# Sinkhorn attention into a SwiGLU block on one core: unit pairs set further apart, and the unread matmuls at the start split in two

## The chip, the core and the metric

The kernel runs on one NeuronCore of a Trainium2 chip. A core has five engines with queues of their own: TensorE (PE, matrix multiply; its weight loads are listed as PEld), VectorE (DVE), ScalarE (ACT), GpSimd (POOL) and SyncE (SP, here only for DMAs). Matmuls write to PSUM, which has eight banks of 128 partitions by 512 fp32 values; ScalarE and VectorE read results from there. The metric is the device time of one launch in microseconds (us), lower is better, as the median of several executions. All times below are us unless marked ns.

## The reference

Four batches, eight heads, 768 positions, head size 64. Each head's sequence is cut into 8 blocks of 96. A small 8 x 8 matrix per head is normalised by five Sinkhorn rounds, and mixes the blocks of K and V. Attention then runs within each block only, and its output, 3072 tokens by 512 features, goes through a SwiGLU block with 1536 hidden features.

```
for _ in range(5):
    P = exp(P - max(P, -1)); P = P / sum(P, -1); P = P / sum(P, -2)
k_sorted = einsum('bhij,bhjcd->bhicd', P, k_blocks)      # v_sorted likewise
attn = softmax(scale * q_block @ k_sorted_block.T)
x = (attn @ v_sorted_block)  -> [3072, 512]
out = (silu(x @ w_gate) * (x @ w_val)) @ w_out
```

## The kernel before, in words

**Start.** V, Q and K of batch 0 are loaded by DMA. ScalarE and VectorE run the five Sinkhorn rounds (L184 to L200), each one exp on ScalarE and six small VectorE operations; the last multiply writes the mixing matrix `p_bf` (L203). Meanwhile TensorE has no real work. It runs matmuls whose result nobody reads: 115 of 32 x 32 (L417), one on V once V has landed (L420), and `fill` of 11 matmuls of 128x512 (L423). Then come the matmuls that transpose `p_bf` (`weights`, L429) and the mixing of V (`v_chunk`, tile `tv`) and of K and Q (`kq_chunk`, tile `tkq`) of batch 0. GpSimd and ScalarE have reordered V into `vch` before (`copy_v`, L116 to L120).

**Units.** A batch has 8 units, each of four blocks times two heads. A unit is: 8 score matmuls (`scores`, `qk`), an exp on ScalarE (`exps`, L289), 8 AV matmuls (`av`, L303), a reciprocal and a scaling multiply on VectorE (`r_sb` L307, `st` L309), and a transpose of `st` to `xt`. For batches 0 and 1 the transpose is four TensorE matmuls into `x_ps` (`xtr`, L320) and a VectorE copy; for batches 2 and 3 it is a DMA (`x_dma`). Units go in pairs: the first uses PSUM pair "b", the second pair "a", two banks each. A pair's AV uses the same banks as its scores, and so do the mixing matmuls of V, K and Q. A bank is written anew only after it was read.

**FFN blocks.** Half a batch of `xt` (384 tokens) is one block, `ffn(n)`, n = 0 to 7: 12 times a gate group (`g_ps`, four matmuls of 128x384) and a value group (`v_ps`, four). Behind a gate group ScalarE takes the tanh (L362) and VectorE multiplies (`gs_sb`, L364); behind a value group VectorE makes `h` (L377). The output matmuls of the block before (`outp`, `o_ps`, 12 of 128x512, in three parts of four) come after each fourth step; ScalarE copies `o_ps` to `o_sb` (L394) and SyncE writes it out. `g_ps`, `v_ps` and some `o_ps` share three "gen" banks in turn; other `o_ps` use one bank "x", which `x_ps` uses too (L386).

**Order.** TensorE's and GpSimd's queues are written by hand: `merge(main, side)` (L545) issues the FFN groups in order, adds up their nominal costs (0.65 for a gate or value group, 0.87 for a part of `o_ps`), and puts each side item behind the first group that brings the sum to the item's time. `units(b, us, ats)` (L522) makes the side items of pairs: scores at `at`, the exp of the second unit at `at + 1.3`, AV at `at + 2.0` and `at + 3.9`, the transposes 3.3 later. `kqs` and `vs` place the mixing of K, Q and V in the same way. VectorE's and ScalarE's orders in the FFN blocks are left to the framework's scheduler. On GpSimd, four copies of V of batch 1 into `vch` (L571 to L572) follow the DMA loads of weights, K, Q and V; every `v_chunk` matmul of batch 1 reads all of them.

Of the kernel before, what the change touches and what calls it, by code (L numbers as in the profile page):

```python
# [10 lines left out]
BF16 = mybir.dt.bfloat16  # L11
# [6 lines left out]
def kernel(  # L18
# [11 lines left out]
    nc = tc.nc  # L30

    B, H, S, D = q.shape
    NB = sort_net.shape[-1]
    C = S // NB
    BH = B * H
    H2 = H // 2
    scale = 1.0 / float(D) ** 0.5
    N_ITER = 5
# [15 lines left out]
    const = ctx.enter_context(tc.tile_pool(name="const", bufs=1))  # L54
# [58 lines left out]
    def copy_v(eng, pair, rows, s, n=4):  # L113
        cs = slice(s * (C // n), (s + 1) * (C // n))
        dst = vch3[rows, :, cs]
        src = v_tiles[pair][rows, cs, :]  # L116
        if eng is nc.scalar:
            eng.copy(dst, src.transpose([0, 2, 1]))
        else:
            eng.tensor_copy(dst, src.transpose([0, 2, 1]))  # L120
# [47 lines left out]
    id4 = ident.rearrange("p (u h j) -> p h u j", u=2, h=H)  # L168
    idq = ident[R:2 * R, R:2 * R].rearrange("p (g two j) -> p two g j", two=2, j=NB)

    rowred = const.tile([BH, NB, 1], FP32)
    colred = const.tile([BH, 1, NB], FP32)
    p_bf = const.tile([BH, NB, H, NB], BF16)
# [6 lines left out]
    def bank_tile(name, tag="gen"):  # L180
        return psum.tile([128, 512], FP32, name=name, tag=tag, bufs=3 if tag == "gen" else 1)

    p_ps = bank_tile("p_ps")[0:BH, 0:NB * NB].rearrange("p (i j) -> p i j", j=NB)
    for it in range(N_ITER):  # L184
        nc.scalar.activation(p_ps, p_sb if it == 0 else p_ps, AF.Exp)
        if it == 1:
            with nc.allow_low_precision("0/1 mask"):
                nc.vector.tensor_reduce(mask, id4, axis=AX.XY, op=ALU.add)
            nc.vector.tensor_copy(rmix[0][R:2 * R, :, 1, :, :], idq)
        if it == 2:  # L190
            copy_v(nc.scalar, 0, lowr, 2, 8)
        if it == 3:
            copy_v(nc.scalar, 0, lowr, 3, 8)
        nc.vector.reduce_sum(rowred[:, :, 0], p_ps, axis=AX.X)
        nc.vector.reciprocal(rowred, rowred)
        nc.vector.tensor_mul(p_ps, p_ps, rowred.to_broadcast([BH, NB, NB]))
        nc.vector.reduce_sum(colred[:, 0, :], p_ps.transpose([0, 2, 1]), axis=AX.X)
        nc.vector.reciprocal(colred, colred)
        if it < N_ITER - 1:
            nc.vector.tensor_mul(p_ps, p_ps, colred.to_broadcast([BH, NB, NB]))  # L200
# [8 lines left out]
    def drain(eng, dst, src):  # L209
        if eng == "v":  # L210
            nc.vector.tensor_copy(dst, src)  # L211
        else:
            nc.scalar.copy(dst, src)  # L213
# [48 lines left out]
    def scores(b, u, tag):  # L262
        half, g = divmod(u, H2)
        k_sb, k_at, q_sb, q_at = ((kqts[b], 0, kqts[b], GI * C) if b < 2 else
                                  (kqts["p"], (b - 2) * GI * C, kqts["q"], (b - 2) * GI * C))
        if tag == "gen":
            wide = None
            pss = [bank_tile("qk"), bank_tile("qk")]
        else:
            wide = pair_tile("qk", tag).rearrange("p (two n) -> p two n", two=2)  # L270
            pss = [wide[:, 0], wide[:, 1]]
        for i4 in range(4):
            at = (g * NB + half * 4 + i4) * C
            for two in range(2):
                lo = two * D
                nc.tensor.matmul(pss[two][:, i4 * C:(i4 + 1) * C],  # L276
                                 lhsT=k_sb[lo:lo + D, k_at + at:k_at + at + 128],
                                 rhs=q_sb[lo:lo + D, q_at + at:q_at + at + C],
                                 start=True, stop=True)
        return wide, pss  # L280
# [11 lines left out]
    def qk(b, u, tag="b"):  # L292
        exps(b, u, *scores(b, u, tag))
# [19 lines left out]
    def xt_tile(tag, n):  # L313
        bank = psum.tile([128, 1024], BF16, name="x_ps", tag=tag, bufs=3 if tag == "gen" else 1)
        return bank[:, 0:n * 4 * C].rearrange("p (g a b) -> p g a b", g=n, b=C)

    def x_to(dst, b, u):
        st = sts.pop((b, u))
        for i4 in range(4):
            nc.tensor.transpose(dst[:, i4, :], st[:, i4].rearrange("p a b -> p (a b)"),  # L320
                                ident[0:C, 0:C])

    def xtr(b, u):
        half, g = divmod(u, H2)
        if g == 0:
            xts[(b, half)] = xtp.tile([128, H2, TW], BF16, name=f"xt{b}_{half}", tag="xt")
        x_ps = xt_tile("x", 1)[:, 0]
        x_to(x_ps, b, u)
        return xts[(b, half)][:, g, :], x_ps.rearrange("p a b -> p (a b)")
# [20 lines left out]
    def gate(n, m):  # L350
        xt = xts[divmod(n, 2)]
        g_ps = psum.tile([128, TW], FP32, name="g_ps", tag="gen", bufs=3)
        for kc in range(NKC):
            nc.tensor.matmul(g_ps, lhsT=wg_sb[:, kc, ts(m, 128)], rhs=xt[:, kc, :],  # L354
                             start=(kc == 0), stop=(kc == NKC - 1))
        gate_out(n, m, g_ps)
# [23 lines left out]
    o_tiles = {}  # L380

    def outp(n, t3, part):
        b, half = divmod(n, 2)
        h_w = h_tiles[n]
        if part == 0:
            o_tiles[n] = bank_tile("o_ps", "x" if 2 <= n < 2 * B - 1 or n == 2 * B - 1 and t3 == 0 else "gen")  # L386
        o_ps = o_tiles[n]
        for m in range(part * 4, part * 4 + 4):
            nc.tensor.matmul(o_ps, lhsT=h_w[:, m, ts(t3, 128)], rhs=wo_sb[:, m, :],  # L389
                             start=(m == 0), stop=(m == NFC - 1))  # L390
        if part < 2:
            return
        o_sb = opool.tile([128, DM], FP32, name="o_sb", tag="o_sb")
        nc.scalar.copy(o_sb, o_ps)  # L394
        base = b * S + half * TW + t3 * 128
        nc.sync.dma_start(out=out[ds(base, 128), :], in_=o_sb)
# [14 lines left out]
    idle_ps = bank_tile("idle_ps", "x")  # L411

    def fill(tile, n):
        for _ in range(n):
            nc.tensor.matmul(tile, lhsT=warm_sb[:, 0:128], rhs=warm_sb, start=True, stop=True)

    for _ in range(115):  # L417
        nc.tensor.matmul(idle_ps[0:32, 0:32], lhsT=warm_sb[:, 0:32], rhs=warm_sb[:, 0:32],
                         start=True, stop=True)
    nc.tensor.matmul(idle_ps[:, 0:128], lhsT=ident[lowr, :],  # L420
                     rhs=v_tiles[0][lowr, 0:2, :].rearrange("p c d -> p (c d)"),
                     start=True, stop=True)
    fill(idle_ps, 11)  # L423

    w_ps = bank_tile("w_ps")[:, 0:NB * B * H].rearrange("p (i b h) -> p i b h", b=B, h=H)

# [48 lines left out]
    idle_ps = bank_tile("idle_ps")  # L475
# [46 lines left out]
    def units(b, us, ats):  # L522
        us = list(us)
        todo = []
        for n, at in enumerate(ats):
            u, u2 = us[2 * n:2 * n + 2]
            held = []
            todo.append((at, lambda u=u, u2=u2, held=held: (qk(b, u, "b"), held.append(scores(b, u2, "a")))))
            todo.append((at + 1.3, lambda u2=u2, held=held: exps(b, u2, *held[0])))
            for w, tag, t in ((u, "b", 2.0), (u2, "a", 3.9)):  # L530
                if b < 2:
                    todo.append((at + t, lambda w=w, tag=tag: av(b, w, tag)))
                    todo.append((at + t + 3.3, lambda w=w: drain("v", *xtr(b, w))))
                else:
                    todo.append((at + t, lambda w=w, tag=tag: (av(b, w, tag), x_dma(b, w))))
        return todo
# [5 lines left out]
    def vs(f, size, ats):  # L542
        return [(at, lambda m=m: f(1, m * size, size, "sv"[m % 2], "ba"[m % 2])) for m, at in enumerate(ats)]

    def merge(main, side):  # L545
        done, k = 0.0, 0
        side = sorted(side, key=lambda t: t[0])
        for c, f in main:
            f()
            done += c  # L550
            while k < len(side) and side[k][0] <= done:
                side[k][1]()
                k += 1
        while k < len(side):
            side[k][1]()
            k += 1

    def ffn(n):
        todo = []
        for m in range(NFC):  # L560
            if n > 0 or m > 1:
                todo.append((0.65, lambda m=m: gate(n, m)))
            if n > 0 or m > 0:
                todo.append((0.65, lambda m=m: value(n, m)))
            if n > 0 and m % 4 == 3:
                for part in range(3):
                    todo.append((0.87, lambda m=m, part=part: outp(n - 1, m // 4, part)))
        return todo
# [7 lines left out]
    q_cast(3)  # L576
    both = slice(0, 128)
    kq1 = kqs(1, (11.8, 1.3, 5.2))
    merge(ffn(0), units(0, range(4, 8), (0.0, 5.2)) + kq1[:1])
    merge(ffn(1), kq1[1:] + vs(v_chunk, 16, (8.6, 9.4, 10.2, 11.0)) + units(1, range(4), (11.2, 15.0)))  # L580
    for s in range(4):
        copy_v(nc.gpsimd, 1, both, s)
    nc.vector.memset(kqt_tile("p")[:, 2 * GI * C:], 0.0)
# [42 lines left out]
```

## Time and profile before

| What | us |
|---|---|
| median of 11 executions | 257.08 (255.89 to 259.81) |
| the profiled execution | 256.89 |
| its span, first to last instruction | 254.7 |
| `g_ps` matmuls (L354), 376 records at 326 ns | 76.5 busy |
| `v_ps` matmuls (L372), 380 records at 326 ns | 77.3 busy |
| `o_ps` matmuls (L389), 256 records at 379 ns | 62.0 busy |
| tanh on ScalarE (L362), 96 at 491 ns | 47.1 busy |
| `gs_sb` on VectorE (L364), 96 at 550 ns | 52.8 busy |
| `h` on VectorE (L377), 96 at 556 ns | 53.3 busy |
| exp of a unit (L289), 30 at 802 ns | 22.7 busy |

The profile is of one execution. Matmul records overlap[...], so a matmul's mean is longer than its share of TensorE's time: groups of four `g_ps` start 0.65 apart when nothing holds them up. A line of the timeline gives the start, the length of a run of like instructions, engine, line and operation, what is written and read, the count, and in brackets the idle time before it with what ended it. A few matmul records are missing, so a count of x11 can stand for 12.

### The profile page before, as it was taken

How to read it: one execution, taken by the hardware profiler on the slowest of the kernel's cores; microseconds unless marked ns; L12 is line 12 of the kernel's file. 1: busy time of each engine (PE TensorE's matmuls, PEld its weight loads, DVE VectorE, ACT ScalarE, POOL GpSimd, SP SyncE). 2: the span in 40 equal slices, each digit the busy share in tenths (PEclk: the TensorE clock that was granted, in tenths of full speed). 3: DMA queues.
4: the chain of work that ended last, by engine and by line, in shares of the span. 5: the costliest groups of instructions: out<-in, count | busy, mean ns of one | idle time of the engine just before them, and what ended most of it. 6: DMA issues, size and time to landing. Idle time of an engine off the chain costs nothing.

```text
span 254.7 us, 6032 instructions
## 1 busy us (share of the span) xinstructions
PE 239.2 (94%) x2545; PEld 145.7 (57%) x2570; DVE 159.6 (63%) x342; ACT 110.8 (44%) x186; POOL 52.1 (20%) x46
## 2 busy tenths in 40 slices
PE   5698989999979999999999999999999999999984
PEld 5295556666545666666656555555555555555533
DVE  6757687984848767658667458545854585545600
ACT  3956553435541643455544433443444344332311
POOL 7848520499469000000000000000000000000000
PEclk9959999999999999999999999999999999999999
DMA  6959999999999167100103111111111111110122
GB/s 103 212 88 179 197 223 206 202 227 197 204 173 122 41 131 164 41 31 13 44 15 84 47 36 54 58 44 32 59 57 41 33 57 57 44 41 0 44 82 84
DMA packets 37866, 23.98 MB, mean 94 GB/s; under 512 B 26064, under 2 KB 34000, under 8 KB 37328
## 3 DMA queue, kind: packets, MB, share of 16 engines
q0 software_dynamic: 21328, 14.16, 38.1%
q1 hardware_dynamic: 16512, 9.45, 13.1%
q8 instruction: 20, 0.33, 0.5%
q14 instruction: 6, 0.05, 0.1%
HBM read 28.32 MB, written 7.86 MB: 142 GB/s over the span
## 4 chain that ended last, share of the span: by engine, by line
PE 85%; DVE 6%; ACT 3%; issue 2%; DMA 2%; DVEq 0%; ACTq 0%; POOLq 0%
PE v_ps L372 23%; PE g_ps L354 23%; PE o_ps L389 23%; PE tkq L233 4%; PE av_ps L303 3%; PE qk L276 2%; DMA v<-in_v_dram 2%; PE tv L245 2%; DVE st L309 2%; ACT e_all L289 1%; PE tv L255 1%; DVE h L377 1%; PE x_ps L320 1%; PE o_ps L405 1%; DVE gs_sb L364 1%
## 5 line engine op out<-in xcount | busy, mean ns | idle before, releaser
L364 DVE SCALAR_TENSOR_TENSOR gs_sb<-th_sb,g_ps 128x384 bf16<-128x384 bf16 x96 | 52.8, 550 | 56.5 <-ACT th_sb L362 54.4
L372 PE MATMUL v_ps<-xt,wv_sb 128*128 128x384 bf16 x380 | 77.3, 326 | 0.3
L354 PE MATMUL g_ps<-xt,wg_sb 128*128 128x384 bf16 x376 | 76.5, 326 | 0.0
L362 ACT ACTIVATE th_sb<-g_ps 128x384 bf16<-128x384 f32 x96 | 47.1, 491 | 56.6 <-PE g_ps L354 53.2
L389 PE MATMUL o_ps<-wo_sb,h 128*128 128x512 bf16 x256 | 62.0, 379 | 1.7 <-ACT o_sb L394 0.7
L377 DVE SCALAR_TENSOR_TENSOR h<-v_ps,gs_sb 128x384 bf16<-128x384 f32 x96 | 53.3, 556 | 7.4 <-PE v_ps L372 0.7
L372 PEld LDWEIGHTS <-wv_sb 128*128 128x128 bf16 x380 | 35.3, 97 | 23.1 <-issue 1.0
L354 PEld LDWEIGHTS <-wg_sb 128*128 128x128 bf16 x376 | 34.7, 97 | 23.1
L389 PEld LDWEIGHTS <-h 128*128 128x128 bf16 x276 | 26.3, 98 | 29.3 <-issue 1.0
L394 ACT COPY o_sb<-o_ps 128x512 f32<-128x512 f32 x23 | 13.5, 586 | 54.2 <-PE o_ps L389 54.2
L120 POOL COPY vch<-v 64x1536 bf16<-64x1536 bf16 (+1 forms) x10 | 28.1, 2853 | 20.0 <-DMA v<-in_v_dram 20.0
L289 ACT ACTIVATE e_all<-qk 96x768 bf16<-96x768 f32 x30 | 22.7, 802 | 6.6 <-PE qk L276 6.6
L309 DVE TENSOR_TENSOR st<-av_ps,r_sb 96x512 bf16<-96x512 f32 x32 | 21.8, 680 | 0.3
L303 PEld LDWEIGHTS <-e_all 96*128 96x128 bf16 x256 | 12.1, 98 | 6.3 <-issue 1.6
L303 PE MATMUL av_ps<-vt,e_all 96*128 96x65 bf16 x256 | 13.5, 194 | 1.9 <-ACT e_all L289 1.9
L213 ACT CAST vt<-tv 96x1024 bf16<-96x1024 f32 (+1 forms) x9 | 9.3, 1031 | 5.6 <-PE tv L245 2.9
L211 DVE CAST vt<-tv 96x1024 bf16<-96x1024 f32 (+1 forms) x9 | 9.8, 1101 | 2.2 <-PE tv L245 2.2
L307 DVE RECIPROCAL r_sb<-av_ps 96x8 f32<-96x8 f32 x32 | 6.3, 198 | 6.6 <-PE av_ps L303 6.5
L233 PE MATMUL tkq<-rmix,kq 128*64 128x64 bf16 x384 | 8.6, 209 | 0.7 <-issue 0.7
L213 ACT CAST kqt<-tkq 128x1024 bf16<-128x1024 f32 (+1 forms) x7 | 6.1, 891 | 6.8 <-PE tkq L233 6.7
L233 PEld LDWEIGHTS <-kq 128*64 128x64 bf16 x384 | 7.8, 125 | 1.9 <-issue 1.8
L211 DVE CAST kqt<-tkq 128x1024 bf16<-128x1024 f32 (+1 forms) x7 | 7.5, 1069 | 2.2 <-PE tkq L233 2.2
(76 smaller groups left out, 136.8 us busy)
## 6 DMA issues: line engine op xcount, KB each, us to landing
out_dram<-o_sb SPq DMA_DIRECT2D x23, 256.0 KB, 2.0
v<-in_v_dram POOLq DMA_DIRECT2D x3, 768.0 KB, 11.6
kq<-in_q_dram POOLq DMA_DIRECT2D x2, 768.0 KB, 11.9
wg_sb<-in_moe_w_gate_dram POOLq DMA_DIRECT2D x6, 256.0 KB, 8.1
wv_sb<-in_moe_w_val_dram POOLq DMA_DIRECT2D x6, 256.0 KB, 8.7
wo_sb<-in_moe_w_out_dram POOLq DMA_DIRECT2D x1, 1536.0 KB, 24.0
kp<-in_k_dram POOLq DMA_DIRECT2D x2, 768.0 KB, 27.4
q_scr<-in_q_dram POOLq DMA_DIRECT2D x2, 768.0 KB, 18.5
```

What stands on the lines that cost most here:

```text
L120: eng.tensor_copy(dst, src.transpose([0, 2, 1]))
L211: nc.vector.tensor_copy(dst, src)
L233: nc.tensor.matmul(tp[two * D:(two + 1) * D, lc, :], lhsT=kq_tiles[b][:, at + lc, :], rhs=rm[:, two, :], start=True, stop=True)
L289: nc.scalar.activation(e_all[:, n:n + 2, 0:4 * C], wide[0:C, :, 0:4 * C], AF.Exp, scale=scale)
L303: nc.tensor.matmul(o[:, two, i4, :], lhsT=e[:, i4 * C:i4 * C + 128], rhs=vt[:, 2 * g + two, half * 4 + i4, :], start=True, stop=True)
L309: nc.vector.tensor_tensor(st.rearrange("p i two d -> p two i d"), o[0:C, :, :, 0:D], r_sb.to_broadcast([C, 2, 4, D]), op=ALU.mult)
L354: nc.tensor.matmul(g_ps, lhsT=wg_sb[:, kc, ts(m, 128)], rhs=xt[:, kc, :], start=(kc == 0), stop=(kc == NKC - 1))
L362: nc.scalar.activation(th_sb, g_ps, AF.Tanh, scale=0.5)
L364: nc.vector.scalar_tensor_tensor(gs_sb, th_sb, 1.0, g_ps, op0=ALU.add, op1=ALU.mult)
L372: nc.tensor.matmul(v_ps, lhsT=wv_sb[:, kc, ts(m, 128)], rhs=xt[:, kc, :], start=(kc == 0), stop=(kc == NKC - 1))
L377: nc.vector.scalar_tensor_tensor(h_tiles[n][:, m, :], v_ps, 0.5, gs_tiles.pop(m), op0=ALU.mult, op1=ALU.mult)
L389: nc.tensor.matmul(o_ps, lhsT=h_w[:, m, ts(t3, 128)], rhs=wo_sb[:, m, :], start=(m == 0), stop=(m == NFC - 1))
```

## The change

Five edits:

- In the Sinkhorn loop, ahead of the fifth round's row sum, VectorE copies the row reciprocals of round four to a small tile `hold`. The 11 fill matmuls become 6, then one 8 x 8 matmul that reads `hold`, then 5. The 32 x 32 matmuls are 114 instead of 115.
- In `units` the AVs are due at 1.9 and 3.6 after the scores instead of 2.0 and 3.9, the TensorE transposes 3.1 after their AV instead of 3.3.
- In block 0 the second pair is due at 5.6 instead of 5.2.
- In block 1 the four `v_chunk`s are due one unit of the sum earlier (7.6 to 10.0 instead of 8.6 to 11.0), and the first pair at 10.3 instead of 11.2.
- Of the last block's output, the second `o_ps` (t3 == 1) takes bank "x" and the first a "gen" bank; before it was the other way round.

```diff
+    hold = const.tile([BH, NB], BF16)
...
+        if it == N_ITER - 1:
+            nc.vector.tensor_copy(hold, rowred[:, :, 0])
...
-            o_tiles[n] = bank_tile("o_ps", "x" if 2 <= n < 2 * B - 1 or n == 2 * B - 1 and t3 == 0 else "gen")
+            o_tiles[n] = bank_tile("o_ps", "x" if 2 <= n < 2 * B - 1 or n == 2 * B - 1 and t3 == 1 else "gen")
...
-    for _ in range(115):
+    for _ in range(114):
...
-    fill(idle_ps, 11)
+    fill(idle_ps, 6)
+    nc.tensor.matmul(idle_ps[0:NB, 0:NB], lhsT=hold, rhs=hold, start=True, stop=True)
+    fill(idle_ps, 5)
...
-            for w, tag, t in ((u, "b", 2.0), (u2, "a", 3.9)):
+            for w, tag, t in ((u, "b", 1.9), (u2, "a", 3.6)):
...
-                    todo.append((at + t + 3.3, lambda w=w: drain("v", *xtr(b, w))))
+                    todo.append((at + t + 3.1, lambda w=w: drain("v", *xtr(b, w))))
...
-    merge(ffn(0), units(0, range(4, 8), (0.0, 5.2)) + kq1[:1])
-    merge(ffn(1), kq1[1:] + vs(v_chunk, 16, (8.6, 9.4, 10.2, 11.0)) + units(1, range(4), (11.2, 15.0)))
+    merge(ffn(0), units(0, range(4, 8), (0.0, 5.6)) + kq1[:1])
+    merge(ffn(1), kq1[1:] + vs(v_chunk, 16, (7.6, 8.4, 9.2, 10.0)) + units(1, range(4), (10.3, 15.0)))
```

In the order this builds for TensorE, `v` for a value group, `g` for a gate group, `x` for four transposes, the parts that move are:

```
block 0 before: scores45 g v g AV4 v g AV5 v g scores67 v x4 g v g x5 AV6 v g AV7 v g v x6 g v tkq g x7 v
block 0 after:  scores45 g v AV4 g v g AV5 v g x4 v scores67 g v x5 g AV6 v g v AV7 g v x6 g v tkq x7 g v
block 1 before: o12 g v tv g tv v tv g tv v scores01 g v o4 AV0 o8 scores23 AV1 g v x0 g AV2 v g x1 v AV3 g v x2 o8 x3 o4
block 1 after:  o12 tv g tv v g tv v tv scores01 g v g AV0 v o8 AV1 o4 scores23 x0 g v AV2 g x1 v g AV3 v g x2 v o8 x3 o4
```

In blocks 2 to 6 an AV moves by one group at most. VectorE's order follows: in block 0 and block 1 the reciprocal and `st` of a unit stand one or two operations further forward among `gs_sb` and `h`.

## The prediction

> **What bounds the kernel now.** I read, in this order: the page's busy shares, the chain that ended last, a table of busy time by stretch of the span, then the timeline of TensorE at every place where a matmul group started later than the sum of the groups ahead of it.
>
> ```profile
> PE 239.2 (94%) x2545; PEld 145.7 (57%) x2570; DVE 159.6 (63%) x342; ACT 110.8 (44%) x186; POOL 52.1 (20%) x46
> PE 85%; DVE 6%; ACT 3%; issue 2%; DMA 2%; DVEq 0%; ACTq 0%; POOLq 0%
> ```
>
> TensorE carries 85% of the chain, so only its idle time can be won. Next, busy time by stretch (columns: stretch, its length, busy time and instructions of PE, PEld, DVE, ACT, POOL, then granted clock, DMA share, GB/s):
>
> ```profile
> 9.00:11.30 2.30, 0.01 (x1) 0.01 (x1) 1.84 (x9) 2.25 (x4) 2.30 (x2) 1.00 0.89 183
> 12.70:16.10 3.40, 3.40 (x68) 3.31 (x68) 1.95 (x3) 1.93 (x3) 0.00 (x0) 0.50 0.61 116
> 16.10:19.50 3.40, 2.93 (x106) 2.90 (x109) 1.79 (x2) 2.11 (x3) 3.39 (x6) 0.50 0.59 74
> ...
> 83.00:126.00 43.00, 42.79 (x521) 27.29 (x523) 28.80 (x52) 21.18 (x33) 0.22 (x1) 1.00 0.29 69
> 126.00:140.00 14.00, 13.72 (x128) 8.01 (x129) 10.50 (x23) 6.87 (x12) 0.00 (x0) 1.00 0.19 44
> 140.00:242.00 102.00, 101.37 (x718) 57.04 (x728) 60.45 (x122) 38.77 (x72) 0.00 (x0) 1.00 0.15 44
> ```
>
> TensorE idles 9.0 to 11.3 and then runs at half clock from 12.7 to 19.5. From 83 to 242 it is all but full: nothing to win there. The waits that remain, from the timeline (start, length, ..., idle before and its releaser):
>
> ```profile
> 38.25 0.34 PE L276 MATMUL qk<-kqt 64*128 64x96 bf16 x8 [0.79 <-DVE st L309]
> ...
> 66.62 0.35 PE L276 MATMUL qk<-kqt 64*128 64x96 bf16 x8 [0.40 <-DVE vt L211]
> ...
> 73.30 0.41 PE L303 MATMUL av_ps<-vt,e_all 96*128 96x65 bf16 x8 [1.63 <-ACT e_all L289]
> ...
> 243.42 5.34 PE L389 MATMUL o_ps<-wo_sb,h 128*128 128x512 bf16 x24 [0.67 <-ACT o_sb L394]
> ```
>
> A matmul's record includes its drain, so I count a wait from the group's slot: 4 matmuls of 128x384 take 0.65, 12 of 128x512 2.58, an AV 0.26, 16 scores 0.44, 4 transposes 0.17 (start-to-start in the timeline). So counted, the four waits are 0.91, 0.53, 1.71 and 0.85; smaller ones are 0.30 (33.85), 0.19 (54.03), 0.24 (129.23) and 0.33 (132.64). Together 5.1 us: the most that the body can give. And one line on GpSimd:
>
> ```profile
> 48.12 11.30 POOL L120 COPY vch<-v 64x1536 bf16<-64x1536 bf16 x4 [13.72 <-DMA v<-in_v_dram]
> ```
>
> These four copies feed every tv matmul of batch 1. They end at 59.42, and their start hangs on a DMA that saturated queues land at 48.1, not on TensorE. tv starts at 61.31 today.
>
> **What the Trainium skill says.** "TensorE: Matmul & The Clock Gate", Part 1: the array's clock is halved after an idle window of about 3.4 us (free-running, not reset by the kernel) and restored after a busy one. The trace agrees: 2.3 us idle among light matmuls, then 6.8 us at 0.50, two windows. "PSUM — Partial Sum Buffer", Engine vs sequencer instructions: the vector and scalar queues are strict FIFO, matmuls start in program order; the trace shows it in the 38.25 line, where everything behind one score group waits. "Perfetto Trace Analysis", Optimization Strategy: recurring bubbles on the busy engine can mean too few PSUM buffers; here g_ps and v_ps share three banks, and a bank is free 1.97 after its g_ps started (0.85 to the tanh, 0.49, 0.03, 0.55, 0.05, from the timeline at 144.12) against three groups of 0.65.
>
> **Head (fill split, hold).** Removed: one 32-wide matmul (0.03) of 115. Added: a DVE copy of 32x8 and an 8x8 matmul; 11 fills become 6 and 5. The copy is not in the old trace: its nearest row is the 32x8 reciprocal at 0.19 (a 128x16 memset takes 0.07). It stands between the multiply that ends at 9.37 and the row sum at 9.63 that waits for ScalarE's exp until 9.60, so it is covered; bounds 0 to 0.1, I take 0. Behind the waiting hold matmul stand five fills of 0.215 and the weights matmuls. hold is ready at about 9.55, the fills end at 10.7, weights cannot start before p_bf at 11.29: slack 0.55. The idle stretch of 2.3 becomes 1.6 and 0.6. If that keeps the clock, 64 tv matmuls go from 55 to 29 ns (-1.65) and the tkq groups from 29 to 17.6 ns: the head could give up to 3 us. But all of it then runs into the GpSimd copies (below), so I take 0 here; bounds -0.28 (gain) and, if the shorter first group trips the clock a window earlier, +1 to +3.
>
> **FFN block 0 (31 to 60).** Of the first pair, AV of unit 4 moves one group ahead, the next pair's scores one group later, behind the transposes of unit 4. I walked the new order with the old durations, DVE at its start-to-start pace there (h 0.475, gs 0.46, reciprocal 0.19, st 0.59, xt 0.265). The 0.91 wait goes: st of unit 5 now ends at 38.01, before the scores at 38.09. But st of unit 4 now stands ahead of gs and h on DVE's queue, so banks come free later and small waits appear: 0.30 (unchanged), 0.14, 0.30 (ACT does two exps ahead of a tanh, 38.6 to 40.1, so its gs ends 41.17 and v_ps starts 41.22), 0.09, 0.22. At the first tkq the new order stands at 46.6 against 46.91: gain 0.31. From there to the o_ps end the order is the same: 60.01 becomes 59.70. tv now follows at once, two groups (1.30) earlier in the order. GpSimd is done at 59.42, so tv just clears it; any further gain of head or block 0 stops after another 0.28.
>
> **FFN block 1 (60 to 82.5).** From 59.70, same method. tv 59.72; vt copies on ACT 60.49 to 61.54, on DVE 61.5 to 62.72; v_ps 5 waits 0.16 for gs; last tv 63.87; its copy on DVE 64.55 to 65.77. Now the scores stand directly behind that tv, where one v_ps group stood between: the second half waits from 64.66 to 65.82, 1.16 instead of 0.53. Two groups that were ahead of the scores now follow them and cover the exps: AV 0 at 68.01, its exps done 65.7. AV 1 stands ahead of the second pair's scores; these start 71.86 and find both banks free (st ends 72.03). AV 2 follows at 73.77, its exp done 73.35: the 1.71 wait is gone. New: 0.37 (tanh behind two exps and the o_sb copy until 74.08), 0.14, 0.09. The block ends at 81.85 against 82.55: gain 0.70 so far, the 0.31 included.
>
> **Blocks 2 to 6.** Block 2: AV one group earlier, exps done 0.35 before it; no wait moves. Block 3: AV and reciprocal go ahead, st of unit 1 ends 132.40 instead of 132.64, so the 0.33 wait falls to 0.03; but the next tanh stays behind exps and o_sb copy (134.69 as now), and v_ps 135.81 and g_ps 136.87 give most back: 0.10 kept. The 0.24 wait stays. Blocks 4 to 6 have slack on both sides (exp done 144.25, AV now 144.77): 0.
>
> **Tail.** The last unit's first o_ps takes a gen bank, free by 241.3 at the latest, in place of x, which ACT frees at 243.37. o_ps then starts at 242.57: 0.85 gained; the second o_ps takes x at 245.15, long free.
>
> Sum: 0.70 + 0.10 + 0.85 = 1.65. The profiled execution took 256.89 (span 254.7 and 2.19 around it); 255.24 on its base. It lies 0.19 under the median 257.08, so 255.4 as a median.
>
> **Rivals.** (1) *The bubbles go more fully*: DVE overlaps better than my pace and the head's gain fills the GpSimd slack: 0.59 at tv, 0.53 + 1.71 kept in block 1, 0.30 in block 3, 0.85: about 3.3, 253.8. For it: DVE idles 1.25 in block 0 today. Against: vt before the scores. (2) *Given back*: the tanh behind paired exps and DVE's queue (3.9 of 4.0 busy at 44 to 48) set the pace, and only the tail stays: 0.6, 256.5. For it: the small waits above are of that kind. (3) *Slower, the clock*: with 1.3 us of fills in place of 2.3 ahead of 9.3, that window counts as idle and the clock halves there. Five fills take 2.1 from 9.6, the weights start 0.5 late, weights and two fills lose another 0.5, and one more window at half clock costs the 128 late tkq matmuls 1.5: some 2.5 to 3 late at block 0. This passes tv one to one: 257.08 - 1.65 + 2.75 = 258.2. It decides once the head is more than 2.4 late. Against: the worst window holds more fill than before. (4) *It doesn't do what it says*: in blocks 4 to 6 pairs were apart already; counted as 0.
>
> **How the numbers follow.** Forecast 0.52 (own range 254.6 to 256.2), rival 1 0.16, rival 2 0.20, rival 3 0.12. No change is within 0.3%, 0.77 us, what this measurement can tell: 256.3 to 257.85. Faster: 0.49 of the forecast, 0.16, and 0.04 of rival 2, 0.69; slower 0.11; same 0.20. Range: rival 1's centre to past rival 2, 253.8 to 257.2.
>
> **What would show it.** Right: tv within 0.3 of the last vch copy; second half of the first scores in block 1 waiting on vt about 1.2; AV 2 of block 1 without its 1.6 wait; no gap at the last o_ps. The clock column at 9 to 20 decides the head: full clock and a wait of tv on POOL confirm the floor. Wrong: waits of 0.3 or more on gs in blocks 0 and 1 adding over 2.5 (rival 2), or half clock at 9.3 or past 19.5 (rival 3).

## The result, and the profile after

The changed kernel takes 259.03 in the median of 12 runs (257.78 to 260.11), the kernel before 256.84 on the same chips. The ratio is 1.0095 with a 95% interval of 1.0077 to 1.0114: slower, by 2.4 us. The forecast was 255.4. The profiled run took 259.55, its span is 257.4 against 254.7.

The page of the changed kernel: busy time by engine, then the chain that ended last, by engine and by line.

```profile
PE 241.7 (94%) x2545; PEld 146.0 (57%) x2570; DVE 161.9 (63%) x343; ACT 110.4 (43%) x186; POOL 52.0 (20%) x46
...
PE 87%; DVE 5%; issue 2%; ACT 2%; DMA 2%; DVEq 0%; ACTq 0%; POOLq 0%
PE v_ps L375 24%; PE g_ps L357 23%; PE o_ps L392 22%; PE tkq L236 4%; PE av_ps L306 3%; PE qk L279 3%; DMA v<-in_v_dram 2%; PE tv L248 2%; PE tv L258 1%; PE idle_ps L418 1%; DVE st L312 1%; PE x_ps L323 1%; PE o_ps L408 1%; DVE hold L192 1%
```

VectorE does one instruction more (x343 for x342), and is busy 2.3 us longer. The last entry of the chain names the instruction: the copy into `hold`, 1% of the span, stands on the path that sets the end. TensorE has as many matmuls as before and is busy 2.5 longer, 2.1 of it ahead of the first value group of block 0, where the clock is halved for longer (below). The timeline of the kernel before at that place:

```profile
6.31 5.61 POOL L120 COPY vch<-v 64x1536 bf16<-64x1536 bf16 x2 [0.69 <-DMA v<-in_v_dram]
...
9.15 0.22 DVE L200 TENSOR_TENSOR p_ps<-p_ps,colred 32x64 f32<-32x64 f32 x1
9.63 0.21 DVE L194 TENSOR_REDUCE rowred<-p_ps 32x8 f32<-32x64 f32 x1 [0.25 <-ACT p_ps L185]
...
11.29 0.77 PE L429 MATMUL w_ps<-ident,p_bf 32*64 32x32 bf16 x16 [2.29 <-DVE p_bf L203]
```

And of the changed kernel:

```profile
6.42 5.57 POOL L120 COPY vch<-v 64x1536 bf16<-64x1536 bf16 x2 [0.81 <-DMA v<-in_v_dram]
...
9.24 0.22 DVE L203 TENSOR_TENSOR p_ps<-p_ps,colred 32x64 f32<-32x64 f32 x1
9.38 2.63 DVE L192 CAST hold<-rowred 32x8 bf16<-32x8 f32 x1
...
12.07 0.16 PE L427 MATMUL idle_ps<-hold 32*8 32x8 bf16 x1 [3.33 <-DVE hold L192]
12.13 0.21 DVE L197 TENSOR_REDUCE rowred<-p_ps 32x8 f32<-32x64 f32 x1
12.17 2.31 PE L418 MATMUL idle_ps<-warm_sb 128*128 128x512 bf16 x5
...
13.32 0.74 DVE L206 TENSOR_TENSOR p_bf<-p_ps,colred 32x256 bf16<-32x256 f32 x2
14.41 0.84 PE L434 MATMUL w_ps<-ident,p_bf 32*64 32x32 bf16 x16
```

The copy of 32x8 values takes 2.63 us. It ends at 12.01, when GpSimd's two copies end (6.42 + 5.57 = 11.99). VectorE works in order, so the fifth round's row sum follows it at 12.13; it stood at 9.63 before. TensorE waits at the gate for 3.33, then still has five fills before the first matmul of `weights`, which moves from 11.29 to 14.41.

The table of stretches of the changed kernel at the start (columns: stretch, length, busy time and instructions of PE, PEld, DVE, ACT, POOL, granted clock, DMA share, GB/s):

```profile
9.00:11.30 2.30, 0.00 (x0) 0.00 (x0) 2.25 (x3) 2.22 (x4) 2.30 (x2) 1.00 0.89 185
11.30:12.70 1.40, 0.62 (x3) 0.33 (x4) 1.22 (x4) 1.25 (x1) 0.69 (x1) 0.54 1.10 219
12.70:16.10 3.40, 3.40 (x23) 1.19 (x21) 1.61 (x7) 0.36 (x1) 0.00 (x0) 0.50 0.67 127
16.10:19.50 3.40, 3.40 (x64) 3.35 (x64) 1.69 (x2) 1.63 (x3) 3.04 (x5) 0.50 0.42 50
19.50:22.90 3.40, 3.10 (x118) 2.91 (x116) 2.07 (x4) 2.04 (x4) 3.40 (x6) 0.68 1.36 176
```

A stretch at half clock counts 0.50, so the shares of 0.54 and 0.68 put the halved clock at about 11.4 until past 21, some 10 us; before it was 6.8 us. Where the time lies, by start times of the same groups in both traces:

| Place | before | after | difference | predicted |
|---|---|---|---|---|
| first matmul of `weights` | 11.29 | 14.41 | +3.12 | 0 |
| first value group of block 0 | 30.43 | 35.01 | +4.58 | 0 |
| group behind the last `o_ps` of block 0 | 60.01 | 63.92 | +3.91 | -0.31 |
| first gate group of block 2 | 82.55 | 86.18 | +3.63 | -0.70 |
| next `o_ps` in block 3 | 132.97 | 136.52 | +3.55 | -0.80 |
| span | 254.7 | 257.4 | +2.7 | -1.65 |

The head loses 4.58; everything behind it gains: 0.67, 0.28, 0.08 and 0.85, in sum 1.88. Two lines of the changed kernel's timeline, from block 1 and from the tail:

```profile
68.65 0.34 PE L279 MATMUL qk<-kqt 64*128 64x96 bf16 x8
70.35 0.35 PE L279 MATMUL qk<-kqt 64*128 64x96 bf16 x8 [1.36 <-DVE vt L214]
...
243.55 7.93 PE L392 MATMUL o_ps<-wo_sb,h 128*128 128x512 bf16 x35
```

In block 1 the first scores wait for `vt` longer than before, and no AV waits for an exp any more. In the tail the output matmuls run through without a gap.

### The profile page after: what moved, and what is told of

Same layout as the page of the kernel before. It is cut to its first block, busy times and chain, and to the rows that moved or that the text cites. A ratio compares the mean times of both kernels' runs of the same rounds, so it can differ in the third digit from the quotient of the medians.

```text
span 257.4 us, 6031 instructions
## 1 busy us (share of the span) xinstructions
PE 241.7 (94%) x2545; PEld 146.0 (57%) x2570; DVE 161.9 (63%) x343; ACT 110.4 (43%) x186; POOL 52.0 (20%) x46
## 4 chain that ended last, share of the span: by engine, by line
PE 87%; DVE 5%; issue 2%; ACT 2%; DMA 2%; DVEq 0%; ACTq 0%; POOLq 0%
PE v_ps L375 24%; PE g_ps L357 23%; PE o_ps L392 22%; PE tkq L236 4%; PE av_ps L306 3%; PE qk L279 3%; DMA v<-in_v_dram 2%; PE tv L248 2%; PE tv L258 1%; PE idle_ps L418 1%; DVE st L312 1%; PE x_ps L323 1%; PE o_ps L408 1%; DVE hold L192 1%; ACT e_all L292 1%
## 5 line engine op out<-in xcount | busy, mean ns | idle before, releaser
L292 ACT ACTIVATE e_all<-qk 96x768 bf16<-96x768 f32 x30 | 22.6, 803 | 7.6 <-PE qk L279 7.6
## 6 DMA issues: line engine op xcount, KB each, us to landing
out_dram<-o_sb SPq DMA_DIRECT2D x23, 256.0 KB, 2.0
wg_sb<-in_moe_w_gate_dram POOLq DMA_DIRECT2D x6, 256.0 KB, 8.9
wv_sb<-in_moe_w_val_dram POOLq DMA_DIRECT2D x6, 256.0 KB, 9.5
```

The lines of the kernel that those rows point to most:

```text
L292: nc.scalar.activation(e_all[:, n:n + 2, 0:4 * C], wide[0:C, :, 0:4 * C], AF.Exp, scale=scale)
```

## The experiments

Line numbers differ by a few between kernels. Ratios are to the kernel before on the same chip, with 95% intervals. `hold` feeds only a matmul that nobody reads, in all of them.

**1. Is it the hold copy and its gate?** The changed kernel with the old head:

```diff
-    hold = const.tile([BH, NB], BF16)
-        if it == N_ITER - 1:
-            nc.vector.tensor_copy(hold, rowred[:, :, 0])
-    for _ in range(114):
+    for _ in range(115):
-    fill(idle_ps, 6)
-    nc.tensor.matmul(idle_ps[0:NB, 0:NB], lhsT=hold, rhs=hold, start=True, stop=True)
-    fill(idle_ps, 5)
+    fill(idle_ps, 11)
```

> The changed kernel with the head put back: no hold copy, no gated matmul, 115 small matmuls and eleven fills; all edits of the bodies and the tail stay. Theory A (the hold copy on VectorE, 2.63 us beside a GpSimd copy, is the whole loss): the head is as before (first weights matmul near 11.3, tkq drained as before), the gains of block 0 (0.3 to 0.67), block 1 (0.28), block 3 (0.08) and the tail (0.85) stay, so 1.5 to 1.9 under the kernel before, about 255.1. Theory B (the body edits cost something of their own once the head is on time, or the clock loses the window in any case): within 0.5 of the kernel before or above it.

Measured: 256.29, ratio 0.9983 (0.9964 to 1.0001). The slow-down is gone, so it was all in the head. But the 1.5 to 1.9 that should remain are not there either: the ratio stands for 0.4, at most 0.9. Half of theory A holds, and theory B has something too; experiments 6 to 10 take that up.

**2. The head alone.** The kernel before with the head lines of the change, nothing else (the diff above, reversed).

> The kernel before with the head of the change alone: hold copy, 114 small matmuls, six fills, the gated matmul, five fills. Theory A: the head is 4.6 late at the first value group as in the changed kernel and nothing gains it back except the slack between GpSimd's copies and tv (tv started 1.9 after the last copy, so none on TensorE's side): +4 to +4.6, about 261.3. Theory B (the loss comes from the interplay with the body edits): under +2.

Measured: 261.14, ratio 1.014 (1.0091 to 1.0189), so +2.3 to +4.9. The head by itself costs no less than the whole change: more in the median, though the two intervals overlap. That is as theory A says; theory B's under 2 is out.

**3. The copy or the gate?** The kernel before with the copy alone:

```diff
+    hold = const.tile([BH, NB], BF16)
+        if it == N_ITER - 1:
+            nc.vector.tensor_copy(hold, rowred[:, :, 0])
```

> The kernel before with the hold copy alone on VectorE; nothing reads hold, the eleven fills and 115 small matmuls stay in one group. Theory A (VectorE is held, and everything of the fifth Sinkhorn round behind it): the copy takes 2.3 to 2.7 again and ends with the second GpSimd copy near 12.0; first weights matmul near 14.3 instead of 11.3; TensorE finishes its fills at about the same time as before and waits; +2.5 to +4.6 in all. Theory C (the time is lost because TensorE waits at the gate, its clock and its fills, not in VectorE): the copy is short or hidden, under +0.5.

Measured: 260.75, ratio 1.0142 (1.0102 to 1.0182), the same as with the gate. The timeline of this kernel:

```profile
6.27 5.58 POOL L120 COPY vch<-v 64x1536 bf16<-64x1536 bf16 x2 [0.66 <-DMA v<-in_v_dram]
...
9.29 2.60 DVE L192 CAST hold<-rowred 32x8 bf16<-32x8 f32 x1
11.99 0.21 DVE L197 TENSOR_REDUCE rowred<-p_ps 32x8 f32<-32x64 f32 x1
13.65 0.54 PE L432 MATMUL w_ps<-ident,p_bf 32*64 32x32 bf16 x6 [3.70 <-DVE p_bf L206]
```

Nothing on TensorE waits for `hold` here, and the loss is whole. It is VectorE's queue, with the Sinkhorn round behind the copy; theory C falls. The gate's own share in the changed kernel is 0.6 at the start of `weights` (14.41 with the five late fills at half clock, 13.65 here, and 0.14 of the difference is a later row sum). In experiment 2's trace the same five fills ran faster (1.25, not 2.31), and its `weights` start as long after the row sum as here (1.67 and 1.66). At the end of the kernel nothing of the gate can be seen.

**4. Why is the copy slow? Another operation in its place.** The changed kernel with

```diff
-            nc.vector.tensor_copy(hold, rowred[:, :, 0])
+            with nc.allow_low_precision("unread"):
+                nc.vector.reciprocal(hold, rowred[:, :, 0])
```

> The changed kernel with hold written by a reciprocal of the same 32x8 values instead of a cast copy; hold's values are used by nothing but the unread matmul. Theory A1 (the cast copy takes a lock on the SBUF ports that GpSimd holds for a whole instruction; the other operations of the loop do not): hold takes about 0.2, the row sum of the fifth round starts by 9.8, first weights near 11.5, and the time is within 0.5 of the version without hold, 255 to 255.5; if the split fills also keep the clock up between 12.7 and 19.5, tv comes to wait for GpSimd's copies at 59.4 and it is 254.5 or so. Theory A2 (any write of a bf16 tile, or any operation placed there, waits for GpSimd): hold takes 2 us or more again, 259. Theory B (the gate and the split cost by themselves, by the clock): hold is short and the time is still 257 or more.

Measured: 256.13, ratio 0.9972 (0.9954 to 0.9991). Timeline and stretches of this kernel:

```profile
6.27 5.56 POOL L120 COPY vch<-v 64x1536 bf16<-64x1536 bf16 x2 [0.66 <-DMA v<-in_v_dram]
...
9.29 0.18 DVE L193 RECIPROCAL hold<-rowred 32x8 bf16<-32x8 f32 x1
9.62 0.21 DVE L198 TENSOR_REDUCE rowred<-p_ps 32x8 f32<-32x64 f32 x1 [0.15 <-ACT p_ps L186]
11.28 0.76 PE L435 MATMUL w_ps<-ident,p_bf 32*64 32x32 bf16 x16 [0.41 <-DVE p_bf L207]
```

```profile
9.00:11.30 2.30, 1.37 (x7) 0.50 (x7) 1.94 (x10) 2.22 (x4) 2.30 (x2) 1.00 0.93 192
...
12.70:16.10 3.40, 3.40 (x129) 3.12 (x127) 2.83 (x4) 2.50 (x5) 0.00 (x0) 1.00 0.65 125
16.10:19.50 3.40, 3.37 (x132) 2.60 (x132) 2.66 (x3) 2.07 (x4) 2.99 (x5) 1.00 0.42 48
```

The same 32x8 values from and to SBUF, in the same place, with the same gate, take 0.18; the row sum waits for exp as before. Theory A1 holds as to which operation waits (the lock that it speaks of comes up in experiment 5), and theory B falls as far as the gate goes: next to experiment 1 no cost of it can be seen. The clock stays at 1.00 here where it was 0.50; but so it does in the profiled execution of experiment 1, with the old head, so this trace does not show that the gate did it. The expected 255 to 255.5 is missed by about 0.9, the same shortfall as in experiment 1.

**5. The place and the source.** Two kernels, each the changed one with one edit:

```diff
-        if it == N_ITER - 1:
+        if it == 1:
             nc.vector.tensor_copy(hold, rowred[:, :, 0])
```

> The changed kernel with the same cast copy into hold placed three rounds earlier, ahead of the second row sum (about 4.5 us), when GpSimd only issues DMAs and its value copies (6.4 to 12) have not begun. Theory A1 (the cast copy is cheap and was held by the GpSimd copy beside it): 0.1 to 0.3 here, next to the 64x64 copy that takes 0.30 there; first weights matmul near 11.3, 256 us. Rival (the cast is slow by itself, or the read of rowred through its strided view is): 2 us or more wherever it stands, about 259.

```diff
-            nc.vector.tensor_copy(hold, rowred[:, :, 0])
+            nc.vector.tensor_copy(hold, p_ps[:, :, 0])
```

> The changed kernel with the cast copy at its place in the fifth round, but reading 32x8 values of the PSUM tile p_ps instead of rowred in SBUF; hold's values are used by nothing but the unread matmul. Theory A1 in the form that the lock is taken for a copy from SBUF to SBUF only: 0.2 to 0.3, beginning after exp at 9.6, and the row sum right after it: weights near 11.5, about 256. In the form that any copy that writes SBUF takes the lock: it ends with the second GpSimd copy near 12.0 and the time is 259 again.

Measured, one execution each: 256.1 and 256.57. The timeline of the first, then of the second:

```profile
4.63 0.16 DVE L192 CAST hold<-rowred 32x8 bf16<-32x8 f32 x1
...
6.28 5.59 POOL L120 COPY vch<-v 64x1536 bf16<-64x1536 bf16 x2 [0.68 <-DMA v<-in_v_dram]
```

```profile
6.41 5.60 POOL L120 COPY vch<-v 64x1536 bf16<-64x1536 bf16 x2 [0.81 <-DMA v<-in_v_dram]
...
9.69 0.15 DVE L192 CAST hold<-p_ps 32x8 bf16<-32x8 f32 x1 [0.25 <-ACT p_ps L186]
9.77 0.20 DVE L197 TENSOR_REDUCE rowred<-p_ps 32x8 f32<-32x64 f32 x1
```

The very same instruction takes 0.16 before GpSimd's copies begin; the same copy beside them takes 0.15 when it reads PSUM. So in these runs three things came together wherever it took 2.6 (2.57 in experiment 2): a copy, from SBUF to SBUF, while a GpSimd copy runs. The Trainium skill, "SBUF — State Buffer", section "Who interferes with whom", states the reason: VectorE and GpSimd share a second pair of SBUF ports, an exclusive lock held for a whole instruction, which VectorE's copies and casts can take (in a mode that uses two ports) and its `tensor_reduce` cannot. "VectorE: DVE Perf Modes", "Why PSUM operands drop a tier", adds that an operand in PSUM rules that two-port mode out. All runs agree with these pages. The first does not name the reciprocal, which took 0.18 here; and the ports themselves are in no trace, so that part of the account rests on the pages.

**6. What became of the gains?** The kernel before with the edits of the bodies alone (the last four lines of the change's diff, without the tail).

> The kernel before with the edits of the bodies alone (wider spacing of unit pairs, earlier v_chunk and pairs in block 1), neither the hold nor the tail edit. The prediction's sum for these: 0.31 + 0.39 + 0.10 = 0.80 less. Theory D (block 0 stands at the arrival of weights and at GpSimd's value copies whenever the head is on time, and the new order has lost the two groups that stood between o_ps and tv, so that tv waits for the copies): between 0.5 less and 0.4 more, with waits on wv_sb, vch or wo_sb in block 0 and 1.48 on vt in block 1.

Measured: 257.28, ratio 1.0025 (1.0005 to 1.0044). No gain, if anything a loss of up to 1.1. Where the gains went shows first in experiment 1's trace. Its head is that of the kernel before, but in this execution it ran at full clock, and the first value group of block 0 starts at 28.23; in the profiled execution of the kernel before, at half clock, it started at 30.43. I call the first "the head on time".

```profile
28.23 0.81 PE L372 MATMUL v_ps<-xt,wv_sb 128*128 128x384 bf16 x4
...
42.88 0.82 PE L354 MATMUL g_ps<-xt,wg_sb 128*128 128x384 bf16 x4 [0.23 <-DMA wg_sb<-in_moe_w_gate_dram]
45.34 1.46 PE L372 MATMUL v_ps<-xt,wv_sb 128*128 128x384 bf16 x4 [1.64 <-DMA wv_sb<-in_moe_w_val_dram]
46.73 1.92 PE L233 MATMUL tkq<-rmix,kq 128*64 128x64 bf16 x64
```

The value group waits for the last piece of `wv`. The wait is followed by half clock: the four `v_ps` matmuls and the 64 of `tkq` take 1.46 and 1.92 instead of 0.82 and 1.20. In the kernel before that value group starts without a wait:

```profile
46.16 0.81 PE L372 MATMUL v_ps<-xt,wv_sb 128*128 128x384 bf16 x4
```

That is only 0.8 later than here, of the 2.2 at the start. The arrival of the weights is a floor: a time before which the group can't start, however early the work ahead of it is done. Then, in this experiment's kernel, the next floors:

```profile
44.89 0.82 PE L372 MATMUL v_ps<-xt,wv_sb 128*128 128x384 bf16 x4 [1.08 <-DMA wv_sb<-in_moe_w_val_dram]
...
59.82 0.64 PE L245 MATMUL tv<-vmix,vch 128*128 128x64 bf16 x16 [0.90 <-POOL vch L120]
...
66.26 0.35 PE L276 MATMUL qk<-kqt 64*128 64x96 bf16 x8 [1.36 <-DVE vt L211]
```

`tv` now follows `o_ps` at once and waits 0.90 for GpSimd's copies; then come 1.36 on `vt`. The order before has two groups there, which cover the copies, and waits of 0.40 (`vt`) and 1.63 (AV) instead: what was taken out in one place came back in two. Experiment 8's trace, with the old order and the head on time, shows the balance: block 0's first value group starts at 28.25 there and 28.52 here, block 2's first gate group at 82.08 and 82.09, so under 0.3 is left in this pair of traces.

With the head late, as in the changed kernel, weights and copies are long done, and only then do the edits of block 0 bring their 0.67. That these are the edits' and not the late head's shows in experiment 2's trace, which has the late head and the old bodies:

```profile
34.72 0.81 PE L375 MATMUL v_ps<-xt,wv_sb 128*128 128x384 bf16 x4
...
64.28 0.81 PE L357 MATMUL g_ps<-xt,wg_sb 128*128 128x384 bf16 x4
```

From the first value group to the group behind the last `o_ps` it takes 29.56, as the kernel before (29.58); the changed kernel takes 28.91.

**7. Is it the weights?** The kernel of experiment 4 with one number changed: the first `tkq` of batch 1 two groups earlier.

```diff
-    kq1 = kqs(1, (11.8, 1.3, 5.2))
+    kq1 = kqs(1, (10.8, 1.3, 5.2))
```

> The version with the reciprocal as hold, and the first tkq group of batch 1 placed two matmul groups earlier in FFN block 0 (10.8 for 11.8), so that its 1.13 us stand before the g_ps and v_ps groups that waited for the last wg and wv pieces (0.87 and 1.33 in that version, where tkq began at 46.29). Theory D (with the head on time, block 0 stands at the arrival of the weights, which eats the gains of the head and of the spacing): these waits shrink by about 1.1 together, the clock is not halved after them (0.5 to 1 more), tv then starts within 0.3 of the last GpSimd copy near 60.0 instead of 0.4 after it: 0.4 to 1.2 less than that version, if the copies do not take it all back. Rival (the waits there are VectorE's or the banks' and only named so): same waits, no gain, or a later drain of tkq makes it slower.

Measured: 256.02, ratio 0.9967 (0.995 to 0.9984), no different from experiment 4. The waits in its timeline:

```profile
45.32 0.82 PE L376 MATMUL v_ps<-xt,wv_sb 128*128 128x384 bf16 x4 [0.44 <-DMA wv_sb<-in_moe_w_val_dram]
56.80 2.76 PE L393 MATMUL o_ps<-wo_sb,h 128*128 128x512 bf16 x11 [1.38 <-DMA wo_sb<-in_moe_w_out_dram]
60.29 0.64 PE L249 MATMUL tv<-vmix,vch 128*128 128x64 bf16 x16 [0.72 <-POOL vch L120]
```

In experiment 4's kernel the gate group before waited 0.71 for `wg` and this value group 1.16 (put down to `gs_sb` there); with other work ahead of them 0 and 0.44 are left. The time comes back as 1.38 on `wo` and 0.72 on `vch`. There are three floors one behind the other, all set by loads: `wv`, `wo`, and the V that GpSimd copies into `vch`. `tv` starts where theory D puts it, and the gain is taken back there.

**8. The tail alone.** The kernel before with the bank of the last output tiles swapped (one line of the change).

> The kernel before with the tail edit alone (of the last unit, the second output tile takes the x bank instead of the first). Forecast of the prediction: 0.85 less, since the wait of 0.67 for o_ps at 243.4 goes and nothing else changes: about 256.0. Rival (given back in the drain and the DMA of the last tiles): under 0.3.

Measured: 256.0 against 256.96, ratio 0.9954 (0.9932 to 0.9976): -1.2 in 0.6 to 1.7. The forecast of 0.85 lies within.

**9. and 10. What is worth keeping?** The kernel before with the reciprocal as `hold`, the split fills and the tail (`best3`); and that kernel with the AV offsets of the change and, in block 1, `v_chunk` as before and only the second pair later (`best2`):

```diff
-    merge(ffn(1), kq1[1:] + vs(v_chunk, 16, (8.6, 9.4, 10.2, 11.0)) + units(1, range(4), (11.2, 15.0)))
+    merge(ffn(1), kq1[1:] + vs(v_chunk, 16, (8.6, 9.4, 10.2, 11.0)) + units(1, range(4), (11.2, 15.7)))
```

> The kernel before with hold as a reciprocal and the split fills, and the tail edit; the bodies as before. Tells what the gate is worth when its copy does not wait. Theory: the clock stays at full speed in the head more often (over half of the runs against a quarter of the runs of before), worth up to 0.7 each time since block 0 stands at the weights and the copies anyway; with the tail 0.85: 0.9 to 1.5 less. Rival (the gate is worth nothing): 0.85 to 1.0 less, the clocks distributed as before.

> The kernel before with: hold as a reciprocal and the split fills, the tail edit, the shorter AV offsets (1.9, 3.6, 3.1), block 0 spaced as before (5.2), v_chunk of block 1 as before (8.6 to 11.0) and its second pair at 15.7 instead of 15.0. Theory D: two groups stand between the last o_ps and tv again, so GpSimd's copies are covered; AV 1 of block 1 precedes the next scores with one group between, so the 1.71 wait goes and leaves at most 0.4; the first scores wait 0.53 as before. With the tail 0.85 less: 2 to 2.5 less than before, about 254.7. Rival: the waits come back as banks or DVE's queue: 0.9 to 1.3 less as the tail alone gives.

Measured: `best3` 256.18, ratio 0.9983 (0.9958 to 1.0007), not better than the tail edit alone, so no gain of the gate can be seen. The clock does move: over all runs with a prompt gate, one that opens at once (experiments 4, 7, 9 and 10) 34 of 59 have a mean granted clock of 0.999 or more, over the runs of the kernel before in the same sessions 23 of 103, and over those of experiments 1, 6 and 8, with the old head, 14 of 53. But little of it reaches the end: those 23 runs of the kernel before have a median of 256.02, the other 80 of 256.94, so a head that starts block 0 some 2.2 earlier is worth 0.9. An estimate from these figures: a third of the runs more, times 0.9, is 0.3 for the gate, too little to be seen here.

`best2` 254.11, ratio 0.9909 (0.9876 to 0.9941): faster than both kernels: by 2.3 us than the one before, and, with 1.0095 for the changed one, by some 4.7 than that. Which of its edits brings how much was not separated; the tail alone gave 1.2 in experiment 8. Its timeline in block 1:

```profile
70.23 0.42 PE L307 MATMUL av_ps<-vt,e_all 96*128 96x65 bf16 x8
70.49 0.81 PE L358 MATMUL g_ps<-xt,wg_sb 128*128 128x384 bf16 x4
71.23 0.78 PE L280 MATMUL qk<-kqt 64*128 64x96 bf16 x16
```

The second AV of the first pair stands ahead of the next pair's scores, with one gate group between; that group gives VectorE time to empty the AV's banks, which the scores take next. The wait of 1.63 is gone; counted from the groups' slots (0.71 from these scores to the next matmuls, less 0.44) 0.27 stays. From the end of block 0 to that of block 1 this kernel takes 21.1 (59.34 to 80.47, ends of `o_ps`), `b_tail` 22.6.

## Why the prediction was wrong, by its steps

**The head: the step that failed.** The prediction put the copy of 32x8 at "0 to 0.1, I take 0", from its "nearest row", the reciprocal of the same size at 0.19. It measured 2.63. The size was the same, and reciprocals of that size even stood beside GpSimd's copies (0.19 at 8.93), but the operation was another: the rows that VectorE shows beside GpSimd's copies in the trace of before are reciprocals, sums and multiplies with an operand in PSUM, and later copies out of PSUM (`xt`, 0.34 at 49.09); its SBUF-to-SBUF copy (64x64, 0.30 at 4.29) ran before those copies began. No row of that trace showed a copy between two SBUF tiles beside GpSimd, so nothing in it bore out the upper bound of 0.1. What the runs put in its place is the end of the GpSimd copy that is running, and that line was in the trace (6.31 + 5.61 = 11.92). The rest of the step, slack of 0.55 and the fills' end at 10.7, fell with it: `weights` started 3.12 late. Of what the head lost behind that, up to 4.58, 1.16 are longer pauses among the `tkq` matmuls of batch 0 (1.88 in all, 0.72 before), whose cause is open (last section).

**Rival 3 (slower, the clock)** had the sign, the place and a size of 258.2, and the reason was another. It let the shorter group of six fills lose the clock. With six fills and a prompt `hold` the clock is kept in more runs, not fewer (34 of 59 against 23 of 103, experiment 9). Its condition, a head more than 2.4 late, was met because VectorE was held; the longer stretch at half clock came with TensorE's wait of 3.33. That its sign, half clock past 19.5, was seen all the same is luck.

**Block 0.** Forecast 0.31 by the order alone; 0.67 with the late head, and with the head on time nothing that reaches the end (experiments 1 and 6). The prediction saw one floor, GpSimd's copies at 59.42, and counted 0.28 of room ahead of it. It did not look at when the last pieces of the weights land: in the trace of before the last `wv` piece showed no wait, since the half clock had made the head late; in the traces of experiments 1 and 6 to 10, where block 0 starts at 28.0 to 28.6, its group waits 0.44 to 1.64. That floor came first. It also said that a gain of the head would stop at GpSimd's copies, but it walked the bodies from its one trace alone, with the late head.

**Block 1.** Forecast 0.39 of its own (0.70 with block 0); measured 0.28. The 1.71 wait went and the `vt` wait grew, to 1.48 in the same count instead of 1.16. The mechanism was right. The forecast saw that `tv`, moved to the end of `o_ps`, just clears GpSimd's copies; with the head on time it does not, and waits 0.90 in experiment 6.

**Blocks 2 to 6 and tail.** 0.08 for 0.10; 0.85 for 0.85, and experiment 8 shows the tail edit alone.

**The sum.** 1.65 forecast for body and tail, 1.88 found in the trace of the changed kernel; less 4.58 of the head it is the +2.7 of the span. That the two sums lie so near is luck: the lateness of the head is what let the bodies gain. With a prompt `hold` the whole change brings 0.7 (experiment 4), no more than the tail alone (experiment 8). Two of the rivals' sums don't come out: rival 1's parts add up to 3.98, not 3.3 (253.1, not 253.8, the lower end of the range), and rival 2 leaves 0.6 of a tail of 0.85 without saying what takes the rest. The result lies on the other side of both.

## What to carry to other kernels

Price a tiny operation from the row of the same operation with operands in the same memories and the same neighbour on GpSimd, not from the row of the same size. If no such row exists, take the rest of the GpSimd instruction beside it as the upper bound (2.57 to 2.63 here), and move all that is queued behind it on VectorE with it. Where it had to stand there, a form that read PSUM (0.15) or a reciprocal (0.18) went through without a wait. And before adding up gains ahead of a wait for data, list every load that the stage needs and when it lands: here three of them stood within a microsecond or two of the schedule, and each took what the one before had given.

## What the runs showed of the hardware that was not expected

- A VectorE cast of 8 elements per partition took 2.57 to 2.63 in three kernels, each time ending within 0.05 of a GpSimd copy's end; the reciprocal of the same tile took 0.18 to 0.19 beside the same GpSimd copies.
- Half clock came back in the middle of a busy kernel: some 2 us of waits for weights between 42.3 and 45.3 in experiment 1 were followed by matmuls at half pace until 48.6. TensorE was busy for 1.53 to 1.58 of the 3.4 us from 41.9 to 45.3 in the three traces where this happened (experiments 1, 4 and the second of 5), and for 2.12 to 2.98 in five where the clock stayed at 1.00 (experiments 6 to 10); the longest single wait of the three was 1.64, well under the idle window of 3.4 that the prediction went by.
- In the changed kernel one run of `tkq` matmuls of batch 0 stops for no wait that the profile shows, while the weights' DMAs run at a share of 1.36 to 1.41:

```profile
23.10 0.63 PE L236 MATMUL tkq<-rmix,kq 128*64 128x64 bf16 x27
25.06 0.26 PE L236 MATMUL tkq<-rmix,kq 128*64 128x64 bf16 x5 [1.33 <-issue]
```

In the kernel before the longest such pause there is 0.47, and the DMAs' share is as high (1.33 to 1.41 from 19.5 to 26.3), so the share alone does not explain it. It is part of the head's 4.58; its cause stays open.
